# A first product of 512 columns in two streams of accumulations, and a subtraction split over two engines

## The chip, the cores and the metric

The kernel runs on one core of a Trainium2 chip. The metric is the device time of one execution in microseconds (us); lower is better. TensorE is called PE in the profile, VectorE DVE, ScalarE ACT, GpSimd POOL and the engine that issues the transfers SP.

## The reference

Three layers follow each other for a batch of 4, 448 tokens and 768 channels (12 heads of 64): an attention with heads mixed before and after the softmax, a gated layer ("first layer" below), and the layer that the change is in ("second layer"):

```python
def _moe2_ref(x, w_theta, w_tok_r, w_tok_i, w_ch):
    theta = x @ w_theta
    zr, zi = x * np.cos(theta), x * np.sin(theta)
    yr = np.einsum('ts,bsd->btd', w_tok_r, zr)
    yi = np.einsum('ts,bsd->btd', w_tok_i, zi)
    u = x + yr + yi
    return (u + np.maximum(u @ w_ch, 0.0)).astype(np.float32)
```

Weights are given in double precision to the kernel and are decoded on the chip.

## The kernel before, in words

Every matrix product of the two layers is made of three products of a 32-bit type (F32R): each operand is split into a high part (a copy by ScalarE, `cast`) and a low part (the operand less its high part, `rest`, by VectorE or GpSimd), and high by high, high by low and low by high are summed in a bank of PSUM. `mm` (L440) issues such a list of terms; the stationary operand has 128 columns, the moving one 384, 448 or 512.

The second layer works on "chunks" of 128 tokens, 14 in all, and on whole batches:

- `load_x2` and `split_x2` (L911, L930) bring a chunk of x2, the output of the first layer, from memory and split it in two halves of 384 elements, e = 0 and 1: ScalarE makes the high part of each half, GpSimd the low part (`x2s`).
- `theta` (L948) multiplies it by w_theta: per chunk two accumulations of 18 products of 384 columns, and after the first six transposes of the raw chunk (L960). Terms 0 to 8 read the first half of the split chunk, terms 9 to 17 the second.
- `angles` and `rotate` (L966, L982) make sine and cosine (VectorE L972 to L976, ScalarE L977 to L979) and the products z = x cos, x sin (VectorE L994, L998); ScalarE makes z's high part and GpSimd its low part.
- `tok` (L1008) multiplies z by w_tok: for each batch six accumulations (k = 0 to 5) of 21 products of 448 columns; VectorE adds the residual (L1021), and ScalarE and VectorE split the sum u.
- `ch` (L1029) multiplies u by w_ch: for each batch six accumulations (m = 0 to 5) of 18 products of 448 columns; GpSimd puts u together again (L1039), and VectorE adds it to the result (L1041).

The order of the work is written out by hand. `U` appends a unit to a list, `d.pre(i, ...)` and `d.post(i, ...)` hang work before and after unit i, and `step` issues it in that order; each engine runs its own instructions strictly in the order of issue. The units of the second layer are: theta of batch 0 and of the first chunk of batch 1, tok of batch 0, then for b = 1, 2, 3 theta of what is left of the batch, ch of b - 1, tok of b, and at the end ch of batch 3. The split of a chunk is hung after theta of the chunk two places ahead, on ScalarE, VectorE and GpSimd alike. In tok of batch 0 VectorE also decodes four pieces of w_ch (L890 to L903).

w_tok lies in seven tiles `wtok0` to `wtok6` of [128, 2, 448], the high part in [:, 0] and the low part in [:, 1], next to each other. u lies in tiles of [128, 512], of which 448 columns are used. `d.ps()` gives a PSUM bank of 512 columns out of eight.

Of the kernel before, what the change touches and what calls it, by code (L numbers as in the profile page):

```python
# [6 lines left out]
F32 = mybir.dt.float32  # L7
F32R = mybir.dt.float32r
# [8 lines left out]
B, H, S, D = 4, 12, 448, 64  # L17
# [361 lines left out]
class Dense:  # L379
# [58 lines left out]
        eng.tensor_tensor(out=out, in0=in_, in1=hi.bitcast(F32), op=ALU.subtract)  # L438

    def mm(self, ps, terms):  # L440
        for i, (l, r) in enumerate(terms):
            self.nc.tensor.matmul(ps, l, r, start=(i == 0), stop=(i == len(terms) - 1))  # L442

    def scratch(self, dram):
        t = lambda name, r, c: dram.tile([2, r, c], F32, name=name)
# [400 lines left out]
def moe2(d, left, win_es, last_u, m1_left):  # L846
    tc, nc, io = d.tc, d.nc, d.io
    wth, wch, wtok, z, x2, st, ut, res = ({} for _ in range(8))
# [14 lines left out]
    def rest():  # L863
# [3 lines left out]
        for name, bufs in (("st", 4), ("x2", 2), ("t2", 2), ("z", 1), ("wtok", 1), ("wch", 1)):  # L867
            d.open(name, bufs, left)

    def load_wtok(c):  # L870
        wtok[divmod(c, 2) if c < 6 else 3] = d.load_pair(d.pools["wtok"], d.wtok_d, slice(128 * c, 128 * c + 128),
                                                        slice(0, S), f"wtok{c}")


    def load_wch(k, half):
# [54 lines left out]
    def split_x2(b, c):  # L930
        raw = x2[b, c][0]
        xh, xl = (d.pools["xp"].tile([128, KD, 128], F32R, tag=f"x2{i}", name="x2s") for i in range(2))
        for e in range(2):
            k = slice(3 * e, 3 * e + 3)
            d.cast(xh[:, k], raw[e])
            d.rest(nc.gpsimd, xl[:, k], raw[e], xh[:, k])
        x2[b, c] += [xh, xl]

    def z_tiles(b, c):
# [68 lines left out]
    def tok(b, k):  # L1008
        if k == 0:
            ut[b] = ([], [])  # L1010
        fs = slice(128 * k, 128 * k + 128)
        ps = d.ps()
        terms = []
        for c in (0, 1, 2, 3) if b % 2 == 0 else (3, 0, 1, 2):
            for ri in range(2 if c < 3 else 1):
                zh, zl = (z[(b, c, ri, hl) if c < 3 else (b, 3, hl)][:, fs] for hl in "hl")
                wh, wl = wtok[(c, ri) if c < 3 else 3]
                terms += [(zh, wh), (zh, wl), (zl, wh)]
        d.mm(ps[:, :S], terms)
        x = res.pop(("x", b, k))  # L1020
        nc.vector.tensor_tensor(out=x, in0=ps[:, :S], in1=x, op=ALU.add)  # L1021
        uh, ul = (d.pools["x"].tile([128, 512], F32R, tag=f"x{i}{k}", name="u") for i in range(2))
        uh, ul = uh[:, :S], ul[:, :S]
        d.cast(uh, x)
        d.rest(nc.vector, ul, x, uh)
        ut[b][0].append(uh)
        ut[b][1].append(ul)

    def ch(b, m):  # L1029
        uh, ul = ut[b]  # L1030
        half, o = divmod(128 * m, 384)
        fs = slice(o, o + 128)
        ps = d.ps()
        terms = []
        for k in range(KD):
            wh, wl = wch[k, half]
            terms += [(wh[:, fs], uh[k]), (wl[:, fs], uh[k]), (wh[:, fs], ul[k])]
        u = d.stage(S, "uu")
        nc.gpsimd.tensor_tensor(out=u, in0=uh[m].bitcast(F32), in1=ul[m].bitcast(F32), op=ALU.add)  # L1039
        d.mm(ps[:, :S], terms)  # L1040
        nc.vector.scalar_tensor_tensor(out=u, in0=ps[:, :S], scalar=0.0, in1=u, op0=ALU.max, op1=ALU.add)  # L1041
        res["o", b, m] = u
# [19 lines left out]
    for b in range(B):  # L1062
        cs = (0, 1, 2, 3) if b % 2 == 0 else (0, 1, 2)
        theta_units(b, cs if b != 1 else cs[1:])
        if b == 0:
            theta_units(1, (0,))
        if b:
            for m in range(KD):
                U(ch, b - 1, m)
        k0 = len(d.units)  # L1070
        if b == 0:
            tok0 = k0
        for k in range(KD):
            U(tok, b, k)
        for k in range(KD):
            d.pre(k0 + k - 1, load_res, b, k)
    for m in range(KD):
        U(ch, B - 1, m)
    for i, (b, c, i0) in enumerate(chunks):
        if i < 2:  # L1080
            d.pre(first - 9 + i, load_x2, b, c, True)
            d.pre(first - 6 + i, split_x2, b, c)
        else:
            i2 = chunks[i - 2][2]
            d.pre(i2 + 1 if i > 3 else first, load_x2, b, c)
            d.post(i2 + 1, split_x2, b, c)
    for i in range(7):
        d.pre(first + 1 + i, load_wtok, i)
    words = [(k, half) for half in range(2) for k in range(KC, KD)]
    for j, kh in enumerate(words):  # L1090
        i = tok0 - 1 + (3 * j + 1) // 2
# [21 lines left out]
def build(tc, nc, io, out):  # L1113
    with tc.manual_schedule(), ExitStack() as top:
        dram = top.enter_context(tc.tile_pool(name="scratch", bufs=1, space=bass.MemoryType.DRAM))
        xT = dram.tile([DM, B * S], F32, name="xT")
        x2T = dram.tile([DM, B * S], F32, name="x2T")
        d = Dense(tc, nc, io, xT, x2T, out)
        d.scratch(dram)
        right, left1, left2 = ExitStack(), ExitStack(), ExitStack()  # L1120
        tail, win_es, last_u, end = moe1(d, left1, right)
        th_es = moe2(d, left2, win_es, last_u, left1)
        for i in range(4):
            tail.setdefault(-2 + 2 * i, []).append(d.step)
        slots = top.enter_context(ExitStack())
        d.open_slots(slots)
        jobs = []
        for half, ks in ((1, range(KD)), (0, range(KE))):
            for k in ks:
                jobs += d.decode_tiles(io["w_in"], slice(128 * k, 128 * k + 128), HF * half, HF * half + HF,  # L1130
                                       lambda k=k, half=half: d.pieces(k, half))
        attention(tc, nc, io, xT, B, jobs, tail)
        while d.at < len(d.units):
            d.step()
        th_es.close()
        right.close()
        slots.close()
        left2.close()
# [69 lines left out]
```

## Time and profile before

| what | value |
|---|---|
| time of three runs | 859.33, 861.32, 862.06 us; median 861.32 |
| profiled execution | 860.64 us, of which the span of its instructions 858.8 us |
| busy share of the span | PE 98%, DVE 69%, ACT 58%, POOL 24% |
| granted clock of TensorE, mean | 1.000 |
| products of the second layer with w_tok, w_theta, w_ch | 504, 504, 432 |

How to read it. A busy PE is not a PE at its peak: the time of a product in the profile, about 368 ns, overlaps that of the next, so the pace of a stream is the distance between the starts of its products, which a row of the timeline gives as the start of one group, the start of the next, and the number of products between. The first column of the timeline is the start in us from the first instruction, the second the length of the group. The time in brackets at its end is what the engine stood idle just before, and which engine and line ended that. The chain of work that ended last is followed back from the last instruction, at each step to what released it.

### The profile page before, as it was taken

To read this page: it belongs to the slowest core of one execution; us is meant where nothing else is said; L and a number is where in the kernel's file an instruction comes from. 1 tells how busy PE (TensorE), PEld (TensorE's weight loads), DVE (VectorE), ACT (ScalarE), POOL (GpSimd) and SP (SyncE) were. 2 spreads that over 40 slices of the span, in tenths; PEclk is the share of its full clock that TensorE was granted. 3 is DMA by queue.
4 is the path that set the end of the run, shared out by engine and by line. 5 is a ranking of instruction groups with operands and counts; after the bars stand their busy time and mean duration, and the time that the engine had idled before them with its cause. 6 is when DMAs were issued, how large, how long until landed. Compare 5 with 4: busy or idle time off the path is not lost.

```text
span 858.8 us, 27171 instructions
## 1 busy us (share of the span) xinstructions
PE 841.4 (98%) x10984; PEld 663.2 (77%) x10984; DVE 591.3 (69%) x1364; ACT 493.8 (58%) x1106; POOL 205.5 (24%) x404
## 2 busy tenths in 40 slices
PE   8999999999999999999999999999999999999998
PEld 2466666556666666798989989899999999999997
DVE  4566667667766767879999998789784287247231
ACT  3788788778887876484846667246443155025010
POOL 0222223223222221000000000038237047306321
PEclk9999999999999999999999999999999999999999
DMA  5666667576767546432857857996511221300301
GB/s 193 211 213 200 211 212 231 164 231 206 236 174 236 184 156 185 144 124 73 275 164 232 290 182 238 372 289 214 194 38 62 67 56 30 118 19 1 118 11 65
DMA packets 108877, 142.16 MB, mean 166 GB/s; under 512 B 25680, under 2 KB 94800, under 8 KB 108752
## 3 DMA queue, kind: packets, MB, share of 16 engines
q1 hardware_dynamic: 108752, 140.42, 51.6%
q8 instruction: 87, 1.43, 0.7%
q14 instruction: 38, 0.31, 0.1%
HBM read 74.26 MB, written 27.59 MB: 119 GB/s over the span
## 4 chain that ended last, share of the span: by engine, by line
PE 87%; DVE 4%; issue 3%; ACT 3%; DMA 2%; SPq 0%; POOL 0%; ACTq 0%; DVEq 0%; POOLq 0%
PE ps L442 51%; PE psB L156 9%; PE psD L242 8%; PE psA L130 7%; PE psC L201 7%; PE psD L246 3%; PE psC L206 1%; DMA blk<-s 1%; DMA wch<-wch_d 1%; PE ps L960 1%; DMA x<-x2T 1%; ACT s L137 0%; ACT u L435 0%; ACT e L170 0%; DVE u L438 0%
## 5 line engine op out<-in xcount | busy, mean ns | idle before, releaser
L170 ACT ACTIVATE e<-psB,nmx 128x448 f32<-128x448 f32 x180 | 112.5, 630 | 50.8 <-DVE nmx L162 48.3
L162 DVE TENSOR_REDUCE nmx<-psB 128x1 f32<-128x448 f32 x180 | 104.0, 619 | 26.9 <-PE psB L156 25.3
L442 PE MATMUL ps<-wtok,z 128*128 128x448 f32 x504 | 104.8, 368 | 0.0
L242 PEld LDWEIGHTS psD<-at,v 128*64 128x64 f32 x1152 | 56.1, 136 | 60.1 <-issue 39.4
L442 PEld LDWEIGHTS ps<-wtok,z 128*128 128x128 f32 x504 | 94.6, 188 | 9.5
L156 PE MATMUL psB<-blk,kpre 64*64 64x448 f32 x720 | 98.5, 541 | 2.6 <-DMA blk<-s 1.2
L130 PE MATMUL psA<-k,q 64*64 64x448 f32 (+2 forms) x768 | 93.1, 542 | 4.5 <-ACT s L137 3.1
L442 PE MATMUL ps<-wth,x2s 128*128 128x384 f32 x504 | 94.3, 342 | 2.4 <-POOL x2s L438 1.9
L438 POOL TENSOR_TENSOR x2s<-x,x2s 128x384 fp32r<-128x384 f32 x28 | 29.1, 1061 | 278.2 <-DMA wch_d<-dh 201.5
L137 ACT ACTIVATE s<-psA 124x896 f32<-124x896 f32 (+1 forms) x90 | 82.7, 919 | 18.7 <-PE psA L130 11.3
L442 PEld LDWEIGHTS ps<-wth,x2s 128*128 128x128 f32 x504 | 88.1, 188 | 4.2 <-POOL x2s L438 3.2
L442 PE MATMUL ps<-u,wch 128*128 128x448 f32 x432 | 89.9, 368 | 0.0
L442 PEld LDWEIGHTS ps<-u,wch 128*128 128x128 f32 x432 | 81.0, 188 | 8.1
L201 PE MATMUL psC<-wr,e 64*64 64x60 f32 x4320 | 82.1, 219 | 2.3 <-issue 1.8
L201 PEld LDWEIGHTS psC<-wr,e 64*64 64x64 f32 x4320 | 72.9, 135 | 9.0 <-POOL wr L188 5.4
L438 POOL TENSOR_TENSOR z<-zz,z 128x384 fp32r<-128x384 f32 x56 | 64.1, 1165 | 55.3 <-ACT z L435 55.1
L242 PE MATMUL psD<-at,v 128*64 128x120 f32 (+1 forms) x1152 | 77.0, 268 | 0.0
L435 ACT ACTIVATE u<-xres 128x448 fp32r<-128x448 f32 x24 | 13.9, 577 | 99.1 <-DVE xres L1021 99.1
L156 PEld LDWEIGHTS psB<-blk,kpre 64*64 64x64 f32 x720 | 36.5, 132 | 44.0 <-issue 19.6
L176 POOL TENSOR_SCALAR rc<-sum 128x2 f32<-128x2 f32 (+1 forms) x92 | 18.1, 196 | 206.9 <-ACT e L170 206.9
L188 POOL TENSOR_SCALAR wr<-wts,rc 128x60 f32<-128x60 f32 x180 | 54.4, 317 | 45.5 <-DVE rc L181 33.2
L442 PE MATMUL ps<-slot,x 128*128 128x512 f32 x252 | 60.1, 396 | 0.0
(111 smaller groups left out, 1435.1 us busy)
## 6 DMA issues: line engine op xcount, KB each, us to landing
blk<-s SPq DMA_DIRECT2D x176, 210.0 KB
draw<-in_w_in SPq DMA_DIRECT2D x24, 256.0 KB
k<-in_kvT SPq DMA_DIRECT2D x24, 224.0 KB
xraw<-xT SPq DMA_DIRECT2D x24, 224.0 KB
xres<-xT SPq DMA_DIRECT2D x24, 224.0 KB
x2T<-xres SPq DMA_DIRECT2D x24, 224.0 KB
xres<-x2T SPq DMA_DIRECT2D x24, 224.0 KB
out<-uu SPq DMA_DIRECT2D x24, 224.0 KB
```

The source lines that it names most:

```text
L130: nc.tensor.matmul(ps[e][r, :S], q[p, o + r.start:o + r.stop], k[p], start=True, stop=True)
L137: nc.scalar.activation(out=out, in_=pair[:m, :, :S], func=AF.Copy, scale=0.125)
L156: nc.tensor.matmul(ps[e][c:c + 64, :S], kpre[k, e], blk[k], start=True, stop=True)
L162: nc.vector.tensor_reduce(out=nmx[r][:, e:e + 1], in_=ps[:, :S], axis=AX.X, op=ALU.max, negate=True)
L170: nc.scalar.activation(out=x, in_=ps[:, :S], func=AF.Exp, bias=m[:, e:e + 1], accum_out=sm[:, e:e + 1])
L176: nc.gpsimd.tensor_scalar(out=rc[:, :m], in0=sm[:, :m], scalar1=1e-9, scalar2=1.0, op0=ALU.add, op1=ALU.mult)
L188: nc.gpsimd.tensor_scalar(out=w, in0=wts, scalar1=rc[:, e:e + 1], scalar2=0.0, op0=ALU.mult, op1=ALU.add)
L201: nc.tensor.matmul(pc[r][h][c:c + 64, o:o + H], x[p, 128 * jc + c:128 * jc + c + 64], w[p], start=(e == 0 and jc == 0), stop=(not two and ...
L242: nc.tensor.matmul(ps[p], v[:, jc, p], main[:, H * jc + 2 * c + i], start=(o == 0 and jc == 0), stop=False)
L246: nc.tensor.matmul(px[p] if e else ps[p, 0], v[q, 3, p], rest[q, 2 * c + i], start=(o == 0 and e == 1), stop=(o > TI))
L438: eng.tensor_tensor(out=out, in0=in_, in1=hi.bitcast(F32), op=ALU.subtract)
L442: self.nc.tensor.matmul(ps, l, r, start=(i == 0), stop=(i == len(terms) - 1))
```

## The change

1. `mm` now skips a term that is `None`. `ch` issues its first term itself, with the whole tile of 512 columns of u (`wide_u`) as moving operand and all 512 columns of the PSUM bank as output; the other 17 terms are as before. `tok` does the same for all accumulations of batches 0, 1 and 3 and for the first of batch 2; there the 512 columns are the 448 of the high part of `wtok0` (even batches) or `wtok6` (odd ones) and the first 64 of its low part. Columns 448 to 511 of the bank are never read.
2. For the wide product of `ch`, GpSimd fills the last 64 columns of u's first tile with zeros, once per batch.
3. In `split_x2` the low part of the first half is made by VectorE, that of the second by GpSimd, in the place of both by GpSimd.

```diff
     def mm(self, ps, terms):
-        for i, (l, r) in enumerate(terms):
-            self.nc.tensor.matmul(ps, l, r, start=(i == 0), stop=(i == len(terms) - 1))
+        for i, t in enumerate(terms):
+            if t:
+                self.nc.tensor.matmul(ps, *t, start=(i == 0), stop=(i == len(terms) - 1))
...
+    first_w = {}
+
     def load_wtok(c):
-        wtok[divmod(c, 2) if c < 6 else 3] = d.load_pair(d.pools["wtok"], d.wtok_d, slice(128 * c, 128 * c + 128),
-                                                        slice(0, S), f"wtok{c}")
+        t = d.pools["wtok"].tile([128, 2, S], F32R, tag=f"wtok{c}", name="wtok")
+        nc.sync.dma_start(out=t.bitcast(F32), in_=d.wtok_d[:, 128 * c:128 * c + 128].rearrange("i p c -> p i c"))
+        wtok[divmod(c, 2) if c < 6 else 3] = t[:, 0], t[:, 1]
+        if c in (0, 6):
+            first_w[c // 6] = t.rearrange("p i s -> p (i s)")[:, :512]
...
             d.cast(xh[:, k], raw[e])
-            d.rest(nc.gpsimd, xl[:, k], raw[e], xh[:, k])
+            d.rest((nc.vector, nc.gpsimd)[e], xl[:, k], raw[e], xh[:, k])
...
+        if b != 2 or k == 0:
+            nc.tensor.matmul(ps, terms[0][0], first_w[b % 2], start=True, stop=False)
+            terms[0] = None
         d.mm(ps[:, :S], terms)
...
         uh, ul = (d.pools["x"].tile([128, 512], F32R, tag=f"x{i}{k}", name="u") for i in range(2))
+        if k == 0:
+            nc.gpsimd.memset(uh[:, S:].bitcast(F32), 0.0)
+            wide_u[b] = uh
...
+        nc.tensor.matmul(ps, terms[0][0], wide_u[b], start=True, stop=False)
+        terms[0] = None
         d.mm(ps[:, :S], terms)
```

PE, the first accumulation of ch for batch 0 and the start of the second: before (the names with numbers are the decoded pieces of w_ch).

```order
L442 MATMUL ps<-u,wch_0_10547 128x448 x3
L442 MATMUL ps<-u,wch_0_10580 128x448 x3
L442 MATMUL ps<-u,wch_0_10624 128x448 x3
L442 MATMUL ps<-u,wch_0_10668 128x448 x3
L442 MATMUL ps<-u,wch 128x448 x6
L442 MATMUL ps<-u,wch_0_10547 128x448 x3
```

The same place of PE in the change:

```order
L1054 MATMUL ps<-u,wch_0_10547 128x512
L443 MATMUL ps<-u,wch_0_10547 128x448 x2
L443 MATMUL ps<-u,wch_0_10581 128x448 x3
L443 MATMUL ps<-u,wch_0_10625 128x448 x3
L443 MATMUL ps<-u,wch_0_10669 128x448 x3
L443 MATMUL ps<-u,wch 128x448 x6
L1054 MATMUL ps<-u,wch_0_10547 128x512
```

The first of the eighteen has become 64 columns wider and comes from another line; nothing has moved.

POOL, the splits of five chunks of x2 (`x_10063` is chunk 2 of batch 0, `x_10066` chunk 3, `x_10295` and `x_10392` the first two of batch 1) with the low parts of z between them: before.

```order
L438 TENSOR_TENSOR x2s<-x_10063,x2s 128x384 x2
L438 TENSOR_TENSOR z<-zz,z 128x384 x4
L438 TENSOR_TENSOR x2s<-x_10066,x2s 128x384 x2
L438 TENSOR_TENSOR z<-zz,z 128x384 x4
L438 TENSOR_TENSOR x2s<-x_10295,x2s 128x384 x2
L438 TENSOR_TENSOR z<-zz,z 128x384 x4
L438 TENSOR_TENSOR x2s<-x_10392,x2s 128x384 x2
```

The same place of POOL in the change:

```order
L438 TENSOR_TENSOR x2s<-x_10063,x2s 128x384
L438 TENSOR_TENSOR z<-zz,z 128x384 x4
L438 TENSOR_TENSOR x2s<-x_10066,x2s 128x384
L438 TENSOR_TENSOR z<-zz,z 128x384 x4
L438 TENSOR_TENSOR x2s<-x_10295,x2s 128x384
L438 TENSOR_TENSOR z<-zz,z 128x384 x4
L438 TENSOR_TENSOR x2s<-x_10392,x2s 128x384
```

Of each pair one is left. The other stands on DVE now. DVE around the split of `x_10295`, before:

```order
L975 SCALAR_TENSOR_TENSOR r<-n,r 128x384
L976 TENSOR_SCALAR r<-r 128x384
L998 TENSOR_TENSOR zz<-ps,n 128x384
L998 TENSOR_TENSOR zz<-ps,r 128x384
L972 TENSOR_SCALAR n<-ps 128x384
L974 SCALAR_TENSOR_TENSOR r<-n,ps 128x384
L975 SCALAR_TENSOR_TENSOR r<-n,r 128x384
```

The same place of DVE in the change:

```order
L981 SCALAR_TENSOR_TENSOR r<-n,r 128x384
L982 TENSOR_SCALAR r<-r 128x384
L1004 TENSOR_TENSOR zz<-ps,n 128x384
L1004 TENSOR_TENSOR zz<-ps,r 128x384
L438 TENSOR_TENSOR x2s<-x_10295,x2s 128x384
L978 TENSOR_SCALAR n<-ps 128x384
L980 SCALAR_TENSOR_TENSOR r<-n,ps 128x384
```

The subtraction stands behind the two products z of the chunk before, and ahead of the first step of the next angles.

## Rows read from the trace of the kernel before

**Rows 1.** The page, shares of the engines and of the chain that ended last.
```profile
PE 841.4 (98%) x10984; PEld 663.2 (77%) x10984; DVE 591.3 (69%) x1364; ACT 493.8 (58%) x1106; POOL 205.5 (24%) x404
...
PE 87%; DVE 4%; issue 3%; ACT 3%; DMA 2%; SPq 0%; POOL 0%; ACTq 0%; DVEq 0%; POOLq 0%
```

**Rows 2.** Table by stretch: length, busy us of PE, PEld, DVE, ACT, POOL; clock, DMA.
```profile
560.00:597.00 37.00, 35.10 (x205) 33.44 (x204) 33.45 (x58) 22.16 (x47) 21.71 (x20) 1.00 0.79 249
...
687.00:715.00 28.00, 28.00 (x169) 27.86 (x168) 23.50 (x39) 16.60 (x35) 15.33 (x14) 1.00 0.22 57
```

**Rows 3.** Timeline of PE, second layer: start, length, line, tiles, columns, count.
```profile
660.95 26.20 PE L442 MATMUL ps<-wtok,z 128*128 128x448 f32 x126
686.99 3.34 PE L442 MATMUL ps<-wth,x2s 128*128 128x384 f32 x18
...
715.04 22.47 PE L442 MATMUL ps<-u,wch 128*128 128x448 f32 x108
737.36 26.20 PE L442 MATMUL ps<-wtok,z 128*128 128x448 f32 x126
```

**Rows 4.** Timeline of PE, first layer.
```profile
439.69 14.86 PE L442 MATMUL ps<-slot,x 128*128 128x512 f32 x63
454.39 2.01 PE L442 MATMUL ps<-x,slot 128*128 128x448 f32 x9
456.24 1.98 PE L442 MATMUL ps<-x,win 128*128 128x448 f32 x9
...
505.33 7.44 PE L442 MATMUL ps<-g,wout 128*128 128x448 f32 x36
512.61 1.98 PE L442 MATMUL ps<-x,slot 128*128 128x448 f32 x9
...
516.27 1.97 PE L442 MATMUL ps<-x,slot 128*128 128x448 f32 x9
518.08 2.00 PE L442 MATMUL ps<-x,win 128*128 128x448 f32 x9
```

**Rows 5.** Who waited for whom, 555 to 640 us: us, times, longest.
```profile
PE ps L442 <- POOL x2s L438: 1.9, 4, 0.7
...
PE ps L442 <- DVE r L974: 0.5, 1, 0.5
```

**Rows 6.** Timeline of PE, 574 to 592 us, with its waits.
```profile
576.50 1.50 PE L442 MATMUL ps<-wth,x2s 128*128 128x384 f32 x7 [0.45 <-POOL x2s L438]
...
582.46 3.09 PE L442 MATMUL ps<-wth,x2s 128*128 128x384 f32 x16 [0.27 <-POOL x2s L438]
...
590.43 1.85 PE L442 MATMUL ps<-wth,x2s 128*128 128x384 f32 x9 [0.71 <-POOL x2s L438]
```

**Rows 7.** The chain that ended last, 585 to 612 us: start, length, what.
```profile
589.42 0.97 POOL x2s L438
...
598.15 6.36 DMA wch<-wch_d
...
605.91 1.25 DVE ch L890
```

**Rows 8.** Timeline of POOL, 572 to 592 us.
```profile
581.38 1.99 POOL L438 TENSOR_TENSOR x2s<-x,x2s 128x384 fp32r<-128x384 f32 x2
...
589.38 1.98 POOL L438 TENSOR_TENSOR x2s<-x,x2s 128x384 fp32r<-128x384 f32 x2
```

**Rows 9.** Timeline of DVE, 572 to 592 us.
```profile
575.03 0.56 DVE L975 SCALAR_TENSOR_TENSOR r<-n,r 128x384 f32<-128x384 int32 x1
...
588.93 0.54 DVE L998 TENSOR_TENSOR zz<-ps,r 128x384 f32<-128x384 f32 x1
...
590.55 1.21 DVE L975 SCALAR_TENSOR_TENSOR r<-n,r 128x384 f32<-128x384 int32 x1
```

**Rows 10.** Timeline of DVE, 604 to 619 us.
```profile
605.91 1.24 DVE L890 TENSOR_SCALAR ch<-ch 128x384 uint32<-128x384 uint32 x1 [1.86 <-ACT ch L888]
...
614.33 0.55 DVE L438 TENSOR_TENSOR ch<-ch,wch 128x384 f32<-128x384 f32 x1
```

More of the change, by code (lines that the diff above doesn't have):

```diff
@@ L1027, in tok @@
         ut[b][1].append(ul)
+    wide_u = {}
     def ch(b, m):
```

## The prediction

> **What bounds the kernel now.** First the shares of the whole execution: PE is busy for 98% of the span and carries 87% of the chain of work that ended last [rows 1], so what counts is how fast TensorE gets through its products and where it waits. Then the table by stretch: the granted clock is 1.00, which is the level of 2.4 GHz, in the first theta stretch (560 to 597 us) as in a later one (687 to 715), but TensorE is busy for only 35.10 of 37 us in the first and for all 28.00 in the other [rows 2]. The reader should see two separate questions: a *pace* (how many ns from one product to the next where nothing waits) and a few *waits* before 636 us. After that the timeline of PE shows products and no wait, up to the last one.
>
> The pace comes from that timeline. In the second layer 126 products with w_tok run from 660.95 to 686.99, which is 26.04 / 126 = 206.7 ns each, and 108 with w_ch from 715.04 to 737.36, 22.32 / 108 = 206.7 ns [rows 3]. In the first layer the same shape runs at other paces: 36 products with w_out from 505.33 to 512.61 take 202.2 ns each [rows 4]. And the same nine products of u (ps<-x,slot) take (456.24 - 454.39) / 9 = 205.6 ns where they follow products of 512 columns, and (518.08 - 516.27) / 9 = 201.1 ns later, after another entry [rows 4]. So the pace of one and the same stream is not fixed by its shape: it has at least two settled values, and how it was entered decides. A product of 512 columns itself takes (454.39 - 439.69) / 63 = 233.3 ns [rows 4], 26.6 more than one of 448 at 206.7. That is 0.42 ns for each of the 64 columns, so by width alone 448 columns are 186 ns, and each product carries some 20 ns besides, an estimate from these two paces.
>
> **The change, part by part.**
>
> *The wide products: price.* There are 24 accumulations with w_ch (18 products each) and 24 with w_tok (21 each). All of the former and 19 of the latter get a first product of 512 columns. The six of batch 0 with w_tok lie ahead of TensorE's last wait (0.49 us on VectorE's r, the second row of [rows 5]) and six times 26.6 ns, 0.16 us, or what they may save, goes into that wait. So 24 + 12 + 1 = 37 are on the path: 37 x 26.6 = 0.98 us dearer. Bounds from below: a wide product costs nothing extra if the 20 ns besides are lost time that its columns fill (0 us).
>
> *The wide products: what they may give back.* The trace has no wide product inside these streams, so the gain is bounded. Bound on one side: none, as the products with w_ch are entered from 384-column products at 715.04, a change of shape and rhythm, and still run at a mean of 206.7 [rows 3]; also the u products just behind a run of 512 columns are at 205.6 [rows 4]. Bound on the other: a settled pace of 200.0, 6.7 ns less, an estimate one ns under the fastest of these rows, whose nine products may still have been settling. I take 201.1, the nearest row in which an identical stream has been seen in both states [rows 4]: 5.6 ns for each later product. On the path these are 24 x 17 = 408 with w_ch, 12 x 20 = 240 with w_tok and 20 in the one accumulation of batch 2, together 668: 668 x 5.6 = 3.74 us. Less the price: 3.74 - 0.98 = 2.76 us faster. With the pace of w_out (202.2, 4.5 ns) it is 3.0 - 0.98 = 2.0 us, with 200.0 it is 4.5 - 0.98 = 3.5 us.
>
> The page "TensorE: Matmul & The Clock Gate" of the Trainium skill (section "Back-to-back issue gap") gives the spacing of a warm stream as the columns over 2.4 GHz plus 2.5 ns, a function of the width alone: 189.2 ns for 448 columns, 215.8 for 512. By that rule the wide products could only cost, and the sum would be that of the second case below. The rows agree with its difference (26.6 ns) and not with its level (206.7), nor with one pace for one width.
>
> *The 64 columns of zeros.* Four GpSimd memsets of 128x64, each a sixth or less of the work of a 128x384 subtraction of 1.0 us (half of 1.98 at 589.38 [rows 8]), so under 0.2 us each, early in w_tok's stage; w_ch's first product comes five accumulations later. Nothing, unless GpSimd were over a stage late. The wide product of w_tok reads what the same transfer brought in. Nothing.
>
> *x2's low parts.* Fourteen subtractions leave GpSimd's queue (1.0 us each) and enter VectorE's, at the places shown above. One costs 0.55 us on VectorE where GpSimd is idle (614.33, the same shape and operation [rows 10]). What it can win: TensorE waits for GpSimd's x2s four times, 1.9 us together [rows 5]. The wait that ends at 576.50 [rows 6] is for the second half, which stays with GpSimd and waits for a transfer: no gain. The other two, 0.27 and 0.71, are for the first half. The chain of waits goes on from there: GpSimd's x2s at 589.42, TensorE, SP's loads, the transfer that lands at 604.5, ScalarE, and VectorE's decoding of w_ch at 605.91 [rows 7]. So what is won at 590 reaches the end.
>
> But VectorE is full in that stretch (33.45 of 37 us [rows 2]) and GpSimd slows it: L975 takes 0.56 us at 575.03 with GpSimd idle, and 1.21 at 590.55 [rows 9] beside the second x2s of 589.38 [rows 8]. The moved subtraction stands just behind the zz that ends at 589.47 [rows 9], when GpSimd has just begun its next. If it runs at once it is done at 590.0 and TensorE gains 0.3; if it sits out GpSimd's 1.0 us it is done near 590.9 and TensorE loses 0.5. Per chunk VectorE gets 0.55 more to do and loses one such meeting with GpSimd, 1.21 - 0.56 = 0.65: a net of -0.1 in each of the four chunks ahead of 636 us. I take that, 0.4 us faster. The ends are 2.4 faster (all of [rows 5] gone) and 2.5 slower (third case). From 687 us on VectorE has 4.5 us free in 28 [rows 2], and no TensorE wait is there: nothing.
>
> *Sum.* The profiled execution took 860.64 us (span 858.8 and 1.8 around it): 860.64 - 2.76 - 0.4 = 857.5. The median of the three runs is 0.7 above that execution. About 0.3%, 2.6 us, is what a measurement here tells from no change; 857.5 is 0.44% under the median.
>
> **The rivals.**
>
> *The pace stays.* The wide product shifts the rhythm, the stream falls back to 206.7 within a few products, and each has only cost 26.6 ns: 860.64 + 0.98 - 0.4 = 861.2. For it: w_ch and w_tok show 206.7 after every entry that the trace has [rows 3], and u at 454.39 stays slow right behind 512 columns [rows 4]. Against it: u at 516.27, and w_out, which is fast straight behind 512 columns at 505.33 [rows 4] with the same order of operands as w_ch. The Trainium skill's rule of the spacing gives this case.
>
> *Half of it holds.* Only w_ch's stream goes over: 408 x 5.6 = 2.28 us back for the same 0.98: 860.64 - 1.30 - 0.4 = 858.9.
>
> *VectorE becomes the bound: slower.* The moved subtraction reads two SBUF operands beside GpSimd and takes 1.1 us or more, as L975 does at 590.55 (1.21 [rows 9]), in four chunks in a row: 4.4 us more on a queue that is full. VectorE's idle time before 605.91 is 1.86 us [rows 10]; past it everything delays the r that TensorE waits for: 4.4 - 1.86 = 2.5 us. With the pace unchanged: 860.64 + 0.98 + 2.5 = 864.1. It decides from the point where a moved subtraction costs over 1.86 / 4 = 0.47 us net of the meeting it spares. Against it: GpSimd has a quarter less to do per chunk.
>
> The Trainium skill's page "SBUF — State Buffer" (section "SBUF: two separate sides") says that a VectorE operation with two SBUF inputs and a GpSimd operation that reads SBUF share a port pair as an exclusive lock, held for a whole instruction. The trace agrees in kind: 1.21 against 0.56 us.
>
> **How the numbers follow.** The forecast has 0.46, the half 0.10, the unchanged pace 0.33, VectorE 0.11. I put the forecast first because an identical stream is seen at both paces, and not higher because neither of the two streams of the change ever left 206.7. Its own range goes from 854.8 (3.5 and 2.4 us) to 858.7 (2.0 us, nothing from x2). The range for 8 in 10 reaches over the unchanged pace with half a microsecond lost at x2: 854.8 to 862.2; the slower case and a tail of the others lie outside. Faster by over 0.3%: the forecast and 0.04 of the half, 0.50; within: 0.06 and 0.33, 0.39; slower: 0.11.
>
> **What would show it.** In the timeline of PE after 636 us: 18 products of w_ch in 233.3 + 17 x 201.1 ns = 3.65 us instead of 3.72, and 21 of w_tok in 4.26 instead of 4.34. If they take 3.75 and 4.37, the pace stayed. In the x2s group on VectorE a mean near 0.55 speaks for the forecast, over 1.0 for the third rival, and there the wait on r before 636 us would be over 2 us. I am wrong if w_ch and w_tok still run at 206.7, or if the gain comes from before 636 us.

## The result and the profile after

| what | before | after |
|---|---|---|
| median time | 861.69 us (859.33 to 865.25, 10 runs) | 868.33 us (865.46 to 872.67, 10 runs) |
| ratio | | 1.0083, 95% interval 1.0062 to 1.0103 |
| profiled execution, its span | 860.64, 858.8 us | 870.1, 868.3 us |

The kernel is slower by 0.8%, some 7 us. The forecast was 857.5 and the range ended at 862.2, so the time lies outside it, and it is longer than the slowest rival said (864.1).

The first view is the table by stretch, cut where TensorE's work changes: from theta's first product to tok's first in batch 0, from there to ch's first product, and from there to the last product of ch(3). Columns: stretch, length, busy us of PE, PEld, DVE, ACT, POOL, clock, DMA share, GB/s. For the kernel before:

```profile
559.04:597.20 38.16, 36.26 (x212) 34.59 (x210) 34.56 (x60) 22.84 (x49) 22.13 (x21) 1.00 0.78 244
597.20:638.63 41.43, 40.52 (x211) 37.62 (x211) 33.55 (x60) 16.09 (x33) 10.78 (x11) 1.00 0.44 150
638.63:855.10 216.47, 216.47 (x1105) 200.70 (x1104) 101.95 (x167) 59.56 (x122) 84.84 (x76) 1.00 0.17 53
```

and for the changed kernel:

```profile
560.44:602.28 41.84, 38.21 (x211) 34.47 (x210) 31.07 (x58) 20.69 (x44) 15.82 (x14) 1.00 0.72 229
602.28:648.19 45.91, 42.46 (x212) 38.80 (x212) 37.09 (x66) 18.31 (x38) 10.90 (x11) 0.96 0.39 131
648.19:864.58 216.39, 216.39 (x1105) 200.76 (x1104) 101.84 (x174) 59.52 (x122) 77.15 (x72) 1.00 0.17 53
```

Theta of batch 0 takes 3.68 us more, tok(0) with theta of batch 1 takes 4.48 more, and the 216 us after that, where all of the forecast's gain was to lie, 0.08 less. Together 8.1 us; the other 1.4 of the 9.5 between the two profiled executions lie before theta (559.04 against 560.44), in code that the change leaves as it was; over the thirteen traces of this case theta begins anywhere between 557.9 and 564.8, so the lengths of stretches tell more than the moments at which they begin. Note the busy times: VectorE is *less* busy in theta of batch 0 than before (31.07 in 41.84 us, against 34.56 in 38.16). It is not the amount of its work that bounds now.

Who waited for whom, 555 to 645 us of the changed kernel: us in total, times, longest. It answers to [rows 5].

```profile
DVE x2s L438 <- ACT x2s L435: 9.2, 6, 2.1
...
PE ps L443 <- ACT z L435: 2.7, 1, 2.7
PE ps L443 <- ACT x2s L435: 2.2, 2, 1.1
...
PE ps L443 <- POOL z L438: 0.4, 1, 0.4
```

TensorE's waits for GpSimd's x2s are gone, as meant. In their place it waits for ScalarE, and VectorE, which before had no wait for ScalarE's cast of x2s, stands 9.2 us waiting for it in six chunks. The timelines of DVE and ACT over one chunk show how (start, length, line, operation; in brackets the idle time before and what ended it). VectorE:

```profile
579.90 1.06 DVE L982 TENSOR_SCALAR r<-r 128x384 f32<-128x384 f32 x1
...
581.34 0.54 DVE L1004 TENSOR_TENSOR zz<-ps,r 128x384 f32<-128x384 f32 x1
583.85 0.63 DVE L438 TENSOR_TENSOR x2s<-x,x2s 128x384 fp32r<-128x384 f32 x1 [1.96 <-ACT x2s L435]
584.40 0.55 DVE L978 TENSOR_SCALAR n<-ps 128x384 int32<-128x384 f32 x1
```

ScalarE:

```profile
580.99 0.53 ACT L983 ACTIVATE n<-r 128x384 f32<-128x384 f32 x1 [1.25 <-DVE r L982]
...
582.07 0.51 ACT L985 ACTIVATE r<-r 128x384 f32<-128x384 f32 x1
582.48 0.92 ACT L435 ACTIVATE z<-zz 128x384 fp32r<-128x384 f32 x2
583.31 0.92 ACT L435 ACTIVATE x2s<-x 128x384 fp32r<-128x384 f32 x2
...
587.16 0.52 ACT L983 ACTIVATE n<-r 128x384 f32<-128x384 f32 x1 [2.94 <-DVE r L982]
```

Read the two against each other. VectorE ends r at 580.96. Only then can ScalarE begin the absolute value (L983), two sines (L984, L985) and two casts of z, and its cast of x2s comes last, at 583.31. The moved subtraction stands in VectorE's queue right behind zz, so VectorE idles from 581.88 to 583.85. The angles of the next half-chunk (L978 to L982) stand behind the subtraction, and ScalarE needs *their* r: it idles for 2.94 us before 587.16. Two engines that used to overlap take turns. TensorE shows the period (its timeline; start, length, line, shape, count):

```profile
583.87 4.01 PE L443 MATMUL ps<-wth,x2s 128*128 128x384 f32 x18 [1.10 <-ACT x2s L435]
...
593.71 4.00 PE L443 MATMUL ps<-wth,x2s 128*128 128x384 f32 x18 [1.10 <-ACT x2s L435]
...
602.51 3.67 PE L443 MATMUL ps<-wtok,z 128*128 128x448 f32 x17
608.91 0.67 PE L443 MATMUL ps<-wtok,z 128*128 128x448 f32 x2 [2.73 <-ACT z L435]
609.99 0.47 PE L443 MATMUL ps<-wtok,z 128*128 128x448 f32 x1 [0.41 <-POOL z L438]
610.30 0.40 PE L1026 MATMUL ps<-wtok,z 128*128 128x512 f32 x1
...
616.15 0.40 PE L1026 MATMUL ps<-wtok,z 128*128 128x512 f32 x1
...
620.50 0.40 PE L1026 MATMUL ps<-wtok,z 128*128 128x512 f32 x1
```

A chunk now takes 593.71 - 583.87 = 9.84 us; before it took 590.43 - 582.46 = 7.97 [rows 6], and the chunk ahead of that 7.55 (578.41 to 585.96 in the same timeline). The last z is late for tok(0): 2.73 and 0.41 us of wait. The accumulation after it takes 616.15 - 610.30 = 5.85 us, the next one 620.50 - 616.15 = 4.35. The granted clock in two stretches of these says why:

```profile
611.50:615.00 3.50, 3.50 (x12) 3.10 (x11) 2.42 (x6) 3.01 (x7) 1.18 (x2) 0.57 0.19 69
616.00:620.00 4.00, 4.00 (x21) 3.63 (x20) 3.76 (x7) 0.53 (x1) 1.19 (x2) 1.00 0.00 0
```

After TensorE stood idle for 3.1 of the 3.8 us before 610, the chip grants it 0.57 of the clock between 611.5 and 615 (mostly the lower level, 1.2 GHz), and 1.00, the upper one (2.4 GHz), from 616. Nine products of that accumulation start 373 ns apart in place of 207, which is the 5.85 - 4.35 = 1.5 us more.

The wide products, the other half of the change, show two paces in one stretch (timeline of PE, the first products of ch(0) and of three accumulations of tok(1)):

```profile
648.19 0.39 PE L1054 MATMUL ps<-u,wch 128*128 128x512 f32 x1
...
670.26 0.39 PE L1026 MATMUL ps<-wtok,z 128*128 128x512 f32 x1
...
674.55 0.40 PE L1026 MATMUL ps<-wtok,z 128*128 128x512 f32 x1
...
678.90 0.40 PE L1026 MATMUL ps<-wtok,z 128*128 128x512 f32 x1
```

All six accumulations of ch(0) take (670.26 - 648.19) / 6 = 3.68 us instead of 3.72 [rows 3], and the first of tok(1) 4.29 instead of 4.34. The second takes 4.35 and all the rest of tok(1) 4.36: dearer than before. In ch(1) and in ch(2) three accumulations are quick and three slow; tok(2), tok(3) and ch(3) are slow throughout. Below, "quick" is the pace of 202.7 ns from one product of 448 columns to the next and "slow" that of 206.7. Four stretches of such products lie between theta's: tok(0); ch(0) with tok(1); ch(1) with tok(2); and ch(2) with tok(3) and ch(3). The "entry" of a stretch is its first accumulation, right behind theta; a "stage" is one tok or one ch.

### The profile page after: what moved, and what is told of

The parts are those of the page before. It is cut to its first block, busy times and chain, and to the rows that moved or that the text cites. A ratio compares the mean times of both kernels' runs of the same rounds, so it can differ in the third digit from the quotient of the medians.

```text
span 868.3 us, 27167 instructions
## 1 busy us (share of the span) xinstructions
PE 846.7 (98%) x10984; PEld 664.9 (77%) x10984; DVE 592.1 (68%) x1378; ACT 494.0 (57%) x1106; POOL 190.7 (22%) x394
## 4 chain that ended last, share of the span: by engine, by line
PE 85%; DVE 6%; issue 4%; ACT 3%; DMA 2%; SPq 0%; ACTq 0%; POOL 0%; DVEq 0%; POOLq 0%
PE ps L443 49%; PE psB L156 8%; PE psD L242 8%; PE psA L130 7%; PE psC L201 7%; PE psD L246 3%; DMA blk<-s 1%; PE psC L206 1%; DVE r L981 1%; DVE r L980 1%; PE ps L1054 1%; PE ps L966 1%; DVE n L978 1%; DVE r L982 1%; DVE zz L1000 1%
## 5 line engine op out<-in xcount | busy, mean ns | idle before, releaser
L443 PEld LDWEIGHTS ps<-wtok,z 128*128 128x128 f32 x485 | 92.3, 190 | 13.5 <-ACT z L435 3.1
L130 PE MATMUL psA<-k,q 64*64 64x448 f32 (+2 forms) x768 | 95.5, 548 | 3.3 <-ACT s L137 1.8
L443 PE MATMUL ps<-u,wch 128*128 128x448 f32 x408 | 87.3, 366 | 0.0
L443 PEld LDWEIGHTS ps<-u,wch 128*128 128x128 f32 x408 | 76.6, 188 | 7.4
L438 POOL TENSOR_TENSOR x2s<-x,x2s 128x384 fp32r<-128x384 f32 x14 | 14.5, 1033 | 268.7 <-DMA x2T<-xres 202.0
```

Of the source, the lines that this page charges most:

```text
L130: nc.tensor.matmul(ps[e][r, :S], q[p, o + r.start:o + r.stop], k[p], start=True, stop=True)
L443: self.nc.tensor.matmul(ps, *t, start=(i == 0), stop=(i == len(terms) - 1))
```

## The experiments

Theory A says that the loss is the wait in VectorE's queue. It has two rivals: by Theory B the loss is VectorE's and GpSimd's contention, the third rival of the prediction, and by Theory C it comes with the wide products. In the first four runs the kernel before had a median of 862.03 us (23 runs).

**The split of x2 alone.** No wide product, only

```diff
-            d.rest(nc.gpsimd, xl[:, k], raw[e], xh[:, k])
+            d.rest((nc.vector, nc.gpsimd)[e], xl[:, k], raw[e], xh[:, k])
```

> The split of x2's low parts alone, no wide product. Theory A (VectorE, strictly in order, now waits for ScalarE's high part at each chunk, and everything queued behind, above all the angles that free TensorE's banks, comes about 2 us later for each of four chunks): slower than before by 6 to 8 us, ratio 1.007 to 1.010. Theory B (the moved subtraction is slowed by GpSimd over the shared port, VectorE has too much work): the same loss, so this run alone does not tell A from B. Theory C (the loss comes from the wide products, by their extra columns and later waits): within 1 us of before.

Measured: 870.33 us (4 runs), ratio 1.0111 (1.0082 to 1.0141). Its waits from 555 to 645 us:

```profile
DVE x2s L438 <- ACT x2s L435: 9.2, 6, 2.1
...
PE ps L442 <- ACT x2s L435: 2.9, 3, 1.1
PE ps L442 <- ACT z L435: 2.8, 1, 2.8
```

The whole loss is there without a wide product, so it does not come from these, and Theory C falls.

**The wide products alone.** All of the change but that line:

```diff
-            d.rest((nc.vector, nc.gpsimd)[e], xl[:, k], raw[e], xh[:, k])
+            d.rest(nc.gpsimd, xl[:, k], raw[e], xh[:, k])
```

> The wide products alone, all of x2's low parts with GpSimd. Theory A and B: within 0.5 us of before, ratio 0.9995 to 1.0005 (the trace of the change puts the accumulations with w_ch that follow theta near 3.68 us instead of 3.72, and all others 0.02 us above before). Theory C: slower by 5 us or more.

Measured: 861.93 us (12 runs), ratio 1.0006 (0.9982 to 1.0029). From the first product of ch(0) to the last of ch(3) the table by stretch has

```profile
638.11:854.96 216.85, 216.85 (x1105) 200.78 (x1104) 102.41 (x167) 59.54 (x122) 85.03 (x79) 1.00 0.17 53
```

which is 0.38 us more than before. Two accumulations of tok(0) and three each of ch(1) and ch(2) were quick; all others were slow, and those with a wide product cost 3.74 and 4.36 us, 20 ns above the kernel before.

**The wait without the work.** GpSimd keeps both subtractions; VectorE gets one of a single column at the place of the moved one.

```diff
             d.rest(nc.gpsimd, xl[:, k], raw[e], xh[:, k])
+            if e == 0:
+                one = d.pools["xp"].tile([128, 1], F32R, tag="one", name="one")
+                d.rest(nc.vector, one, raw[e][:, 0, :1], xh[:, 0, :1])
```

> The kernel before, all low parts still with GpSimd, and one more subtraction of a single column on VectorE at the place in its queue where the change puts the moved one: it waits for the same high part and does next to no work. Theory A: most of the loss comes back, 5 to 8 us slower than before, with idle time of VectorE of about 2 us ahead of that instruction in the chunks from 575 us on. Theory B: no work was moved, so within 1 us of before.

Measured: 871.13 us (4 runs), ratio 1.0116 (1.0082 to 1.0150). Its waits, and the added subtraction in the timeline of DVE:

```profile
DVE one L438 <- ACT x2s L435: 9.0, 5, 2.1
...
PE ps L442 <- POOL x2s L438: 3.7, 4, 1.5
...
PE ps L442 <- ACT z L435: 3.2, 1, 3.2
```

```profile
583.39 0.24 DVE L438 TENSOR_TENSOR one<-x,x2s 128x1 fp32r<-128x1 f32 x1 [1.96 <-ACT x2s L435]
```

A subtraction that takes 0.24 us on VectorE costs as much as the whole split. The work that was moved is not the price; its place in the queue is. That shows Theory A, and Theory B is not needed. The two losses are not made of the same parts, though: here GpSimd keeps both subtractions, TensorE waits 3.7 us for them (1.9 before), and behind one of these waits the granted clock was 0.62 from 585.58 to 590.03.

**The subtraction placed later.** VectorE's half is issued at another place, behind the next angles (L977 to L981 here), so that ScalarE has its cast done by then; GpSimd keeps the other half.

```diff
+    def rest_x2(b, c):
+        raw, xh, xl = x2[b, c]
+        d.rest(nc.vector, xl[:, :3], raw[0], xh[:, :3])
...
+    for i, (b, c, i0) in enumerate(chunks):
+        if i > 1:
+            d.post(chunks[i - 2][2] + 1, rest_x2, b, c)
```

> No wide products; VectorE makes the low part of the first half, but stands one step of the angles later in its queue (behind the next clamp), where ScalarE's high part has long been there. Theory A: the loss is gone; TensorE waits less for x2s than before (1.9 us there), so 0 to 1.5 us faster than before. Theory B: the same work and the same neighbours on GpSimd, so still slower by 4 us or more.

Measured: 863.21 us (12 runs), ratio 1.0024 (1.0005 to 1.0043): a miss, though by the medians most of the 8 us is back. VectorE's wait for ScalarE's cast falls to 1.5 us, and part of what is left shows in its own timeline:

```profile
584.13 1.37 DVE L438 TENSOR_TENSOR x2s<-x,x2s 128x384 fp32r<-128x384 f32 x1
...
592.75 1.35 DVE L438 TENSOR_TENSOR x2s<-x,x2s 128x384 fp32r<-128x384 f32 x1
```

and in TensorE's:

```profile
575.62 5.22 PE L442 MATMUL ps<-wth,x2s 128*128 128x384 f32 x18 [1.59 <-ACT x2s L435]
...
585.55 3.09 PE L442 MATMUL ps<-wth,x2s 128*128 128x384 f32 x16 [0.53 <-DVE x2s L438]
...
594.15 3.09 PE L442 MATMUL ps<-wth,x2s 128*128 128x384 f32 x16 [1.32 <-DVE x2s L438]
```

Beside GpSimd's subtractions of z (582.64 to 585.08, 591.27 to 593.67) and of x2s behind them the same operation takes 1.35 us instead of 0.55 [rows 10], and TensorE waits for it. So the contention of Theory B is real, though second in size, and stands in the way of this repair. The trace itself shows more: its execution took 865.44 us, above the median, and the two stretches from theta to ch(0) are 4.0 us longer than before (41.06 and 42.55 us). TensorE waits 1.59 us at 575.62 for a cast of ScalarE that waited for its transfer, and then has 0.59 of the clock up to 579.8. The trace of the kernel with 464 columns at the second accumulation (below), which leaves x2 to GpSimd, has such a wait too (1.68 us, and 0.67 of the clock behind it), so that part is not put down to the new place.

For the next four runs the kernel before had a median of 861.95 us (16 runs).

**The split in the late chunks only,** and **only in four chunks around the end of batch 0.** `split_x2` gets a flag per chunk.

```diff
-    def split_x2(b, c):
+    def split_x2(b, c, two=True):
...
-            d.rest(nc.gpsimd, xl[:, k], raw[e], xh[:, k])
+            d.rest((nc.vector, nc.gpsimd)[e or not two], xl[:, k], raw[e], xh[:, k])
...
-            d.post(i2 + 1, split_x2, b, c)
+            d.post(i2 + 1, split_x2, b, c, i > 5)
```

and `i < 6` in the last line for the second kernel.

> The kernel before with x2's split between VectorE and GpSimd only for the last two chunks, (1,2) and (1,3), whose theta lies in the second half of theta b1; the first six chunks as before, no wide products. Theory A (VectorE's queue waits for ScalarE's cast, and this costs where TensorE has no chunk in hand, that is in theta of batch 0 and the entry of tok(0)): within 1 us of the kernel before. If the split costs by the work itself wherever it stands: +2 us or more, a quarter of the 8 us.

> The kernel before with x2's split for chunks 2 to 5 only, (0,2), (0,3), (1,0) and (1,1), no wide products. Theory A: theta of batch 0 and the entry of tok(0) lose as in the full split, so +6 to +9 us, with TensorE's wait of 2 to 3 us on ScalarE's z ahead of tok(0) and its first products at half the rate behind it. If the loss is spread evenly over the chunks: half of it, about +4 us.

The texts on record miscount the chunks: of the 14, the first kernel splits the last eight, (1, 2) and those of batches 2 and 3, not two; an even spread of the loss would be 8/14 of it there, some 5 us, and 4/14, some 2.5 us, in the second.

Measured: 859.05 us (12 runs), ratio 0.9976 (0.9949 to 1.0004) for the late chunks, and 871.47 us (4 runs), ratio 1.0126 (1.0077 to 1.0175) for the four. The loss is tied to the place: eight late chunks cost nothing that can be measured, and four of 14 cost all of it (9.5 us by the medians, half a microsecond over the upper end expected), with a wait of 2.8 us on ScalarE's z ahead of tok(0). The late chunks have the same wait on VectorE, from 640 to 800 us of their trace:

```profile
DVE x2s L438 <- ACT x2s L435: 14.3, 7, 2.4
```

But TensorE waits for nothing there after 645 us: its work in hand covers it. That the late chunks gain something is not shown, though their median is 2.9 us lower: the interval takes in no change, and theta of batch 0, tok(0) and all from ch(0) on take in that trace what they took before, within 0.1 us.

**The width of the wide product.** This run has the wide products alone, with a width of its own for each accumulation from ch(0) and tok(1) on (512 at the entries of ch(0), ch(1) and ch(2), none in tok(0)).

```diff
+        n = WC[b][m]
+        if n:
+            nc.tensor.matmul(ps[:, :n], terms[0][0], wide_u[b][:, :n], start=True, stop=False)
+            terms[0] = None
```

> The kernel before with the wide first product alone (x2 as before), but of another width at each accumulation: 452 to 512 columns in steps of 4 to 8 in the stages tok(1) to tok(3) and in ch(0) to ch(3), none in tok(0). Theory 'entry': the quicker pace (products 202 to 203 ns apart instead of 206.7) is entered only right behind theta, whatever the width; then the accumulations of tok(2), tok(3) and ch(3), which no theta precedes, stay at 206.7 ns at every width. Theory 'width': 512 columns are the wrong size to shift the stream and another one is right; then some accumulation of those stages comes below 205 ns a product at a width that can be read off (w_ch below 3.70 us, w_tok below 4.30 us). Time, by the first theory: 862 us as for the wide products alone.

Measured: 861.2 us (one run). Theory 'entry' falls: tok(2), tok(3) and ch(3) all have quick accumulations. First products of three accumulations of ch(0) in the timeline of PE:

```profile
647.93 0.37 PE L1059 MATMUL ps<-u,wch 128*128 128x460 f32 x1
...
651.65 0.38 PE L1059 MATMUL ps<-u,wch 128*128 128x468 f32 x1
...
655.32 0.37 PE L1059 MATMUL ps<-u,wch 128*128 128x476 f32 x1
```

With 460 columns the accumulation stays slow (651.65 - 647.93 = 3.72 us), with 468 it turns quick (3.67). Over all stages, products of 464, 468, 480 and 488 columns that found the stream slow left it quick 9 times of 9, and one of 456 did too; 460, 496, 504 and 512 left it slow, 7 of 7. A product that found it quick left it quick in 11 of 22 cases, with no width in order (464, 476, 484 and 500 always, 452, 456 and 472 never).

**One wide product per stretch.** 512 columns only at the first accumulation of tok(0), ch(0), ch(1) and ch(2), directly behind theta:

```diff
+WT = ((512, 0, 0, 0, 0, 0), (0, 0, 0, 0, 0, 0), (0, 0, 0, 0, 0, 0), (0, 0, 0, 0, 0, 0))
+WC = ((512, 0, 0, 0, 0, 0), (512, 0, 0, 0, 0, 0), (512, 0, 0, 0, 0, 0), (0, 0, 0, 0, 0, 0))
```

> The kernel before with one wide first product per stage: at the first accumulation of tok(0) and of ch(0), ch(1), ch(2), which stand behind theta; x2 as before. If the product must be repeated to hold the pace, only the first accumulation of a stage is at 203 ns (3.68 us in w_ch, 4.29 us in w_tok) and the next is at 206.7 ns. If the state once entered lasts as long as nothing disturbs it, all six accumulations of ch(0) stay near 203 ns a product, and the repeated wide products of the change bought nothing but 20 ns each lost in the other state. Time: 860 to 862 us.

Measured: 857.32 us (one run). tok(0) is quick to its end; ch(0) with tok(1) is slow throughout; ch(1) with tok(2), and ch(2) with tok(3) and ch(3), are quick to their end. The state lasts, and the repeated products of the change are what ended it there. Timed again beside a kernel before of 860.32 us (29 runs), the reference for the last two runs too:

> The same kernel as wide_first_only (one product of 512 columns at the first accumulation of tok(0), ch(0), ch(1) and ch(2)), timed in more executions. In its one look three of the four stretches stood at 202.7 ns a product to their end, and the time was 857.3 us. If the single wide product decides the pace, the median lies near 858 us (three of four stretches, about 700 products by 4.0 ns, 2.8 us below the 862 of the kernel before). If the pace is chance at the end of theta and the wide product has no say, the time is that of the kernel before within 1 us.

Measured: 859.94 us (12 runs), ratio 0.9985 (0.9959 to 1.0011). The pattern was the same (ch(0) with tok(1) slow, the three others quick), on another chip, and so was the time from ch(0) on:

```profile
638.89:853.16 214.27, 214.27 (x1105) 200.78 (x1104) 103.17 (x167) 59.51 (x122) 84.93 (x79) 1.00 0.17 54
```

That is 2.2 us less than before. The total times of 12 runs can't tell that from nothing; the traces of the two executions can.

**464 columns, once per stretch,** at the second accumulation, and at the first:

```diff
-WT = ((512, 0, 0, 0, 0, 0), (0, 0, 0, 0, 0, 0), (0, 0, 0, 0, 0, 0), (0, 0, 0, 0, 0, 0))
+WT = ((0, 464, 0, 0, 0, 0), (0, 0, 0, 0, 0, 0), (0, 0, 0, 0, 0, 0), (0, 0, 0, 0, 0, 0))
```

with `WC` in the same way, and for the other kernel 464 in the first column of both tables.

> One product of 464 columns, at the second accumulation of tok(0), ch(0), ch(1) and ch(2); no other extra column, x2 as before. In the width sweep every product of 464 to 488 columns that found the stream at 206.7 ns (9 of 9) left it at 202.7 ns, and the two of 464 that found it at 202.7 left it there; 512 never shifted it. Theory 'width': the first accumulation may be at either pace, all after it to the next theta are at 202.7 ns, in all four stretches; 926 products by up to 4.0 ns, 3 to 3.5 us below the kernel before, 858 to 859 us at the median. If the sweep's shifts were chance, some stretches stay at 206.7 ns and the time is near 861 us.

> One product of 464 columns, at the first accumulation of tok(0), ch(0), ch(1) and ch(2), directly behind theta. If the width alone matters, as for the second accumulation: 858 to 859 us. If what matters is that the stream has already settled at 206.7 ns when the product comes, it is no better than 512 columns there: some of the four stretches stay at 206.7 ns.

Measured: 858.41 us (12 runs), ratio 0.9990 (0.9967 to 1.0013) at the second accumulation, where each of the four stretches is slow for one accumulation and quick to its end from then on; and 858.24 us (12 runs), ratio 0.9974 (0.9954 to 0.9993) at the first, where all four are quick from the start, so the doubt in the last expectation falls. In the timeline of PE for the latter:

```profile
640.20 0.37 PE L1059 MATMUL ps<-u,wch 128*128 128x464 f32 x1
640.41 21.85 PE L445 MATMUL ps<-u,wch 128*128 128x448 f32 x107
662.09 25.70 PE L445 MATMUL ps<-wtok,z 128*128 128x448 f32 x126
687.63 3.35 PE L445 MATMUL ps<-wth,x2s 128*128 128x384 f32 x18
```

and in the table by stretch, from the first product of ch(0) to the last of ch(3):

```profile
640.20:853.47 213.27, 213.27 (x1105) 200.76 (x1104) 103.00 (x167) 59.50 (x122) 84.92 (x79) 1.00 0.18 54
```

126 products in 687.63 - 662.09 = 25.54 us are 202.7 ns each; the stretch takes 3.2 us less than the 216.47 before. Of this the medians show 2.1 us, and the interval reaches from 0.6 to 4.0. So this kernel, with four products of 464 columns and x2 left to GpSimd, is faster than both others, by a quarter of a per cent against the kernel before. The medians alone would be thin evidence (the late chunks above came out 2.9 us lower with no stretch shorter); the trace's 3.2 us in the stretch that was acted on carries it.

## Why the prediction was wrong

Two terms of the sum failed. The one for x2's low parts had the wrong place in VectorE's queue and left out the wait there, and this made the kernel slower; the one for what the wide products give back brought next to nothing.

- **x2's low parts: -0.4 us forecast, +8 measured.** The step that failed reads "the moved subtraction stands just behind the zz that ends at 589.47 ... If it runs at once it is done at 590.0". A chunk has two pairs of zz, and the subtraction stands behind the other. The trace of before held its price. Timeline of DVE, then of ACT:

```profile
585.26 0.54 DVE L998 TENSOR_TENSOR zz<-ps,r 128x384 f32<-128x384 f32 x1
585.73 0.54 DVE L972 TENSOR_SCALAR n<-ps 128x384 int32<-128x384 f32 x1
```

```profile
587.23 0.92 ACT L435 ACTIVATE x2s<-x 128x384 fp32r<-128x384 f32 x2
```

  zz ends at 585.80, and the first of the two casts at 587.74: 1.94 us in which VectorE would stand, where the changed kernel has 1.96. At 589.47, where the step put the subtraction, that cast had ended. The step asked what the subtraction takes and not when its input is there, nor what is queued behind it. A chunk grows by 1.87 to 2.3 us (9.84 against 7.97 and 7.55), about the wait of 1.94. A smaller misreading: three of the four waits of [rows 5] were for the first half, as the one that ends at 574.20 (0.47 us) was left out.
- **The bounds of that step.** The slower end, 2.5 us, came from contention alone. The wait is longer than any cost of the work, it comes in each chunk, and its consequences added to it: z was late for tok(0) (3.1 us of wait), and the clock was lower after that (1.5 us). None of these was a term of the sum.
- **VectorE becomes the bound (864.1).** This rival was right that the loss lies ahead of ch(0) and at VectorE, and wrong in its mechanism: x2s on VectorE takes 0.64 us at the median, not over 1.0, and VectorE is idle more than before. The contention shows in one of the 14 in the changed kernel (1.30 us at 614.92, beside GpSimd's z) and in eight of 14 where the subtraction was placed later (1.35 to 1.38 us). The Trainium skill's "SBUF — State Buffer" (section "SBUF: two separate sides") says that such an operation of VectorE (two inputs in SBUF) and one of GpSimd share a port pair under an exclusive lock; these numbers agree with it in kind. The run with a single column shows that the loss does not need it.
- **The wide products: price.** 26.6 ns each forecast. In a slow stream one costs 20 ns net (3.74 against 3.72 us), as the next few products come up to 5 ns closer. The size was about right.
- **The wide products: give-back.** 2.76 us net of the price were forecast (3.74 less 0.98); the changed kernel gained 0.08 us net, and the wide products alone lost 0.38. The idea, that one stream has two settled paces and the entry decides, was right in part: an entry sets the pace, but a product inside the stream can change it too. Two terms failed: the quicker pace is 202.7 ns, not 201.1, which is 4.0 ns a product and not 5.6; and "for each later product" took for granted that repeating the wide product does no harm. A product of 512 columns never turned a slow stream quick inside a stage, and it ended quick ones: of the 37 accumulations with a wide product on the path 13 were quick. By the pace of w_out in [rows 4], 202.2, the size would have been right.
- **The pace stays (861.2).** The wide products by themselves came close to this rival, with the time of the kernel before (ratio 1.0006), but as a mixture of both paces and not at 206.7 throughout. The Trainium skill's "TensorE: Matmul & The Clock Gate" (section "Back-to-back issue gap") has one spacing for one width: the columns over 2.4 GHz plus 2.5 ns, an estimate of 189.2 ns here, which the section calls the gap of an isolated product. These runs show 206.7 and 202.7 ns for the same stream at a granted clock of 1.00, so neither that level nor a single value holds here.
- **The 64 columns of zeros** were forecast at nothing, rightly: no row of the changed kernel has TensorE waiting for them.

## What to carry to other kernels

Before an operation is moved to an engine with time to spare, find in the trace the moment at which its input is ready and the moment at which that engine's queue reaches it: if the first is later, the difference is paid by everything behind it, and where the producer needs what stands behind it, by every round of the loop. It reaches the total time where the engine that bounds has no other work in hand, as in theta of batch 0, and not where it has, as in the late chunks. The share of busy time says nothing of this. And a trick that acts on a state (here the pace of TensorE) should be tried once per entry before it is repeated in every loop.

## What the runs showed that was not expected

- One stream of products with 448 columns has two settled paces, 206.7 and 202.7 ns, that last for more than 200 products at a granted clock of 1.00. Behind theta it was quick in 3 of 29 entries without a wide product, in 15 of 19 with 512 columns, in 4 of 4 with 464 (where TensorE waited at an entry, the pace that it settled at counts). Inside a stretch a single product of 464, 468, 480 or 488 columns turned a slow stream quick each time (13 of 13 with the four at the second accumulation), and 512 columns never did. Each run has one trace, and only one kernel was traced twice (with the same pattern), so how far an entry repeats from execution to execution is open. Theta's products have two paces as well: without any wide product, the eight accumulations of batch 2 took 27.60 us in the run with the added one-column subtraction and 28.05 in the kernel before, both at a granted clock of 1.00. What in the chip holds the paces apart was not found.
- In the four profiled executions with a wait of about 3 us in the first accumulation of tok(0), the granted clock after it was between 0.57 and 0.79 over 3.5 or 4 us, and was 1.00 again from 616 us on; the kernel before, busy throughout there, had 1.00. It fell behind shorter waits in theta as well (0.62 behind 1.55 us, 0.59 behind 1.59), though not behind one of 1.49 us.
- A subtraction of a single column, 0.24 us of work, made the kernel 1.2% slower.
